# Linear attention into a tanh-shrink layer: the loads of the first batch move to a second queue, and the first batch's steps are reordered

## The chip, the cores and the metric

One core of one Trainium2 chip runs the whole program. The metric is the device time of one execution in microseconds (us), from start to end of the program; the kernel before takes 303.34 us (median of 3 runs, 302.98 to 303.97). The profile is one execution of its own, with a span of 301.5 us from its first to its last instruction; all times inside the program below are counted from the start of that span.

## The reference

Eight batches, eight heads, a sequence of 576 and a head size of 64 go through linear attention; its output, 4608 rows of 512, goes through two dense layers.

```python
phi = lambda x: np.where(x > 0, x, np.exp(x) - 1.0) + 1.0
q_p, k_p = phi(q), phi(k)                       # q, k, v: (8, 8, 576, 64) float32
kv  = np.einsum('bhsd,bhse->bhde', k_p, v)
z   = np.sum(k_p, axis=2)
num = np.einsum('bhsd,bhde->bhse', q_p, kv)
den = np.einsum('bhsd,bhd->bhs', q_p, z)[..., None] + 1e-06
x   = (num / den).transpose(0, 2, 1, 3).reshape(4608, 512)
h   = x @ w_in                                  # 512 x 2048
out = (h - np.tanh(h)) @ w_out                  # 2048 x 512
```

## The kernel before, in words

**The dense part.** The 4608 rows are handled in nine chunks `c` of 512. Layer 1 of a chunk is 16 groups `fi`, each of four 128x128 by 128x512 bf16 matmuls (line 275, `l1mm`); ScalarE takes tanh (line 280, `th`) and VectorE subtracts it (line 281, `gT`). Layer 2 is 16 groups of four matmuls (line 290, `l2mm`), which ScalarE copies out (line 295) and the SP queue stores (line 298). Weights and activations on TensorE are bf16.

**The attention part.** The attention of later batches is cut into small steps and hung between those groups, in the lists `s1` (after group `fi` of layer 1) and `s2` (after a quarter of a layer 2 group). The attention of batch 0 can't be hidden that way, since layer 1 of chunk 0 needs it: it is written out in front of the loop, behind 36 dummy matmuls on zeros (line 343) that keep TensorE's clock up. The order is by hand; each engine runs its own instructions in the order of the program, and waits on semaphores for the others.

The steps of batch 0, in the order of the program:

- `load_kq` (lines 85 and 89) and `load_v` (line 104) read q, k and v, which are float32 in memory, and turn them into bf16 on the way; they go out on the GpSimd queue. For batch 0, k and q come in four transfers each: half `i` (0 or 1) of the head pairs, and `hg` 0 or 1, which fill partitions 0 to 63 or 64 to 127. `load_wi` (line 110) and `load_wo` (line 114) bring the weights on the same queue. After the loads of w_in GpSimd builds `sel`, a selection matrix, with four `affine_select` (line 314).
- `phi`: exp on ScalarE (line 127, `e`), `max(x,0)+1` on VectorE (line 128, `r`), and the minimum of the two on VectorE (line 129, `kp` or `qp`): the same as the reference's function. It runs for k half 0, k half 1, q half 0, q half 1.
- `a_qT_pe(0, i)`: nine transposes of `qp` on TensorE (line 152) into two PSUM banks; the first is copied out by ScalarE (line 156), the second by VectorE (line 158).
- `a_kv_half(0, i)`: 18 matmuls (line 165) of kp with v and a column of ones, which give kv and z; VectorE masks them into `kz` (line 182).
- `a_den(0)`: 20 small matmuls (lines 190 and 194) give den, and VectorE takes the reciprocal (line 201, `rden`).
- `a_num_copy(0)`: one matmul per pair of heads `p` for the first 512 columns (line 220) and four small ones for the remaining 64 (line 223); ScalarE copies them to `ns` (lines 244 and 249). Pairs 0 and 2 need only half 0 of `kz` and `qT`, pairs 1 and 3 only half 1.
- `a_spread_pe(0)`: matmuls with `sel` (line 263) spread 1/den over the partitions, for two pairs at a time: pairs 0 and 1 into PSUM banks 0 to 3 (`bp_a`), pairs 2 and 3 into banks 4 to 7 (`bp_b`). They are float32, and each shows as two instructions in the profile.
- `a_scale(0, p)`: VectorE multiplies `ns` by the spread values into `xT` (line 268), the bf16 input of layer 1. Layer 1 of chunk 0 begins with groups `fi` 0 to 3 side by side in banks 0 to 3, all four for p = 0, then for p = 1, and so on, so that it can follow the scaling.

In chunk 1 the transposes of batch 2 hang behind groups 5 and 7 of layer 1, and use banks 6 and 7 (`attn`) in turn.

Of the kernel before, what the change touches and what calls it, by code (L numbers as in the profile page):

```python
# [11 lines left out]
F32 = mybir.dt.float32  # L12
BF16 = mybir.dt.bfloat16
# [5 lines left out]
def kernel(  # L19
# [9 lines left out]
    nc = tc.nc  # L29
    B, H, S, D = q.shape  # L30
# [3 lines left out]
    NP = H // 2  # L34
    NF = DF // 128
    NC = N // 512
    J = S // 64
# [25 lines left out]
    attn = Banks([6, 7])  # L63
# [14 lines left out]
    k_t, q_t = {}, {}  # L78

    def load_kq(b, src, store, name):  # L80
        t = kpool.tile([128, 2, 2, J, D], BF16, name=name)
        for i in range(2) if b == 0 else ():
            for hg in range(2):
                h0 = 4 * hg + 2 * i
                nc.gpsimd.dma_start(  # L85
                    out=t[64 * hg:64 * hg + 64, i].rearrange("p h j d -> p h (j d)"),
                    in_=src[b, h0:h0 + 2].rearrange("h (p j) d -> p h (j d)", j=J))
        for hg in range(2) if b > 0 else ():
            nc.gpsimd.dma_start(  # L89
                out=t[64 * hg:64 * hg + 64].rearrange("p i h j d -> p (i h) (j d)"),  # L90
                in_=src[b, 4 * hg:4 * hg + 4].rearrange("h (p j) d -> p h (j d)", j=J))
        store[b] = t

    def load_k(b):
        load_kq(b, k, k_t, "kraw")
# [4 lines left out]
    def load_v(b):  # L100
        for i in range(2):
            for hg in range(2):
                h0 = 4 * hg + 2 * i
                nc.gpsimd.dma_start(  # L104
                    out=v_b[b % 2][64 * hg:64 * hg + 64, i, 0:2].rearrange("p h j d -> p h (j d)"),
                    in_=v[b, h0:h0 + 2].rearrange("h (p j) d -> p h (j d)", j=J))

    def load_wi(g):
        f0 = g * (DF // 4)
        nc.gpsimd.dma_start(out=w_in_sb[:, :, f0:f0 + DF // 4],  # L110
                            in_=moe_w_in[:, f0:f0 + DF // 4].rearrange("(ko ki) f -> ki ko f", ki=128))
# [31 lines left out]
            out=qT_t[b].rearrange("p i j g t -> p (i j) (g t)"),  # L143
            in_=qp_t[b].rearrange("p i j h d -> p (i j h d)"))

    def a_qT_pe(b, i, banks):
        if i == 0:
            new_qT(b)
        for n, (j0, j1) in enumerate(((0, 5), (5, 9))):
            ps = banks().bitcast(BF16).rearrange("p (j t) -> p j t", t=128)  # L150
            for j in range(j0, j1):
                nc.tensor.transpose(ps[:, j - j0, :], qp_t[b][:, i, j].rearrange("p h d -> p (h d)"), ident)  # L152
            src = ps[:, 0:j1 - j0, :]
            dst = qT_t[b][:, i, j0:j1].rearrange("p j g t -> p j (g t)")
            if n == 0:
                nc.scalar.copy(dst, src)
            else:
                nc.vector.tensor_copy(dst, src)
# [57 lines left out]
    def num_mm(b, p, banks):  # L216
        kz, qT = kz_t[b], qT_t[b]
        ps = banks().rearrange("p (j t) -> p j t", j=8)
        if p < NP:
            nc.tensor.matmul(ps, kz[:, p // 2, p % 2, 0:128], qT[:, p % 2, 0:8, p // 2, :], start=True, stop=True)  # L220
        else:
            for a in range(NP):
                nc.tensor.matmul(ps[:, a, :], kz[:, a // 2, a % 2, 0:128], qT[:, a % 2, 8, a // 2, :],
                                 start=True, stop=True)
        return ps
# [11 lines left out]
                xT[:, :, S * b + 512:S * b + 576].rearrange("p a (t c) -> p a t c", t=4),  # L237
                ps[:, 0:NP, :].rearrange("p a (t c) -> p a t c", t=4), rdb[:, :, :, 8, :])

    def a_num_copy(b, banks):  # L240

        ns = rpool.tile([128, NP, J, 64], F32, name="ns", tag="rdb")
        ps = num_mm(b, NP, banks)
        nc.scalar.copy(ns[:, :, 8, :], ps[:, 0:NP, :])
        if b == 0:
            for p in range(NP):
                num_mm(b, p, banks)
            for p in (0, 2):
                nc.scalar.copy(ns[:, p:p + 2, 0:8, :].rearrange("p a j t -> p a (j t)"),
                               ps_all[:, 4 + p:6 + p, :])  # L250
        else:
            for p in range(NP):
                ps = num_mm(b, p, banks)
                nc.scalar.copy(ns[:, p, 0:8, :], ps)
        return ns

    def a_spread_pe(b, bank0, pairs):

# [45 lines left out]
    nc.scalar.activation(act0, zero[:, 0:1], AF.Exp)  # L304
    load_k(0)
    load_q(0)
    load_v(0)
    make_identity(nc, ident)
    for g in range(4):
        load_wi(g)  # L310
    nc.gpsimd.memset(sel, 0.0)
    for t in range(4):
        r = slice(32 * t, 32 * t + 32)
        nc.gpsimd.affine_select(
            out=sel[r], in_=sel[r], compare_op=ALU.not_equal, fill=1.0, base=0,
            channel_multiplier=1, pattern=[[-1, NP], [-4, 2], [0, 64]])
    load_k(1)
    load_wo(0)
    load_q(1)
# [19 lines left out]
        rest -= part  # L339


    for n in range(36):
        nc.tensor.matmul(ps_all[:, n % 4, :], zero[:, 0:128], zero, start=True, stop=True)  # L343
    for i in range(2):
        a_kphi(0, i)
# [3 lines left out]
    a_qT_pe(0, 0, side)  # L349
    a_kv_half(0, 0, kvb)  # L350
    a_qT_pe(0, 1, side)
    a_kv_half(0, 1, kvb)
    a_den(0, Banks([0]))
    ns0 = a_num_copy(0, Banks([1, 4, 5, 6, 7]))
    bp_a = a_spread_pe(0, 0, (0, 1))
    bp_b = a_spread_pe(0, 4, (2, 3))
    for p in range(NP):
        a_scale(0, p, ns0, (bp_a, bp_b)[p // 2], 144 * (p % 2))
    load_q(2)
    load_k(2)  # L360
    load_v(2)
# [1 line left out]
    for c in range(NC):  # L363
        gT = gpool.tile([128, NF, 512], BF16, name="gT")
        n1, n2 = c + 1, c + 2
        s1 = {i: [] for i in range(16)}
        s2 = {i: [] for i in range(16)}
        if c == 0:
            side = Banks([4, 5, 6, 7])
            sub = {}  # L370

            def spread1(h):
                sub["bp"] = a_spread_pe(1, 4, (2 * h, 2 * h + 1))
                for p in (2 * h, 2 * h + 1):
                    a_scale(1, p, sub["ns"], sub["bp"], 144 * (p % 2))

            s1[11].append(lambda: a_kphi(1, 0))
            s1[13].append(lambda: a_kphi(1, 1))
            s1[15].append(lambda: a_qphi(1, 0))
            s2[1].append(lambda: a_qphi(1, 1))  # L380
            s2[4].append(lambda: a_qT_pe(1, 0, side))
            s2[5].append(lambda: a_qT_pe(1, 1, side))
            s2[6].append(lambda: a_kv(1, side))
            s2[8].append(lambda: a_den(1, side))
            s2[9].append(lambda: (sub.update(ns=a_num_copy(1, side)), load_v(3)))
            s2[11].append(lambda: spread1(0))
            s2[13].append(lambda: spread1(1))
            s2[14].append(lambda: a_qphi(2, 0))
            s2[15].append(lambda: a_qphi(2, 1))
        elif n1 < B:  # L390
            s1[9 if c == 1 else 5].append(lambda: a_kv(n1, attn))
            s1[11 if c == 1 else 8].append(lambda: (a_den(n1, attn), a_spread(n1)))
            for p in range(NP + 1):
                s2[9 + p].append(lambda p=p: a_num(n1, p))
            if c + 3 < B:
                s1[10].append(lambda: load_v(c + 3))
        if c == 1:
            s1[1].append(lambda: a_kphi(2, 0))
            s1[3].append(lambda: (a_kphi(2, 1), load_k(3), load_q(3)))
            s1[5].append(lambda: a_qT_pe(2, 0, attn))  # L400
            s1[7].append(lambda: a_qT_pe(2, 1, attn))
        if c >= 1 and n2 < B:
            if c > 1:

                s1[0].append(lambda: (gate(gT, 0), load_k(n2), load_q(n2)))
            d = 4 if c == 1 else 2
            s2[d].append(lambda: a_kphi(n2, 0))
            s2[d + 2].append(lambda: a_kphi(n2, 1))
            s2[d + 4].append(lambda: a_qphi(n2, 0))
            s2[d + 6].append(lambda: (a_qphi(n2, 1), a_qT_dma(n2)))  # L410
        if c == 0:

            hs = [ps_all[:, fi, :] for fi in range(4)]
            first = Banks([4, 5, 6, 7, 0, 1, 2, 3])
            for p in range(NP):
                for fi in range(4):
                    l1mm(c, fi, hs[fi], p)
            for fi in range(4):
                l1act(fi, hs[fi], gT)
        for fi in range(4 if c == 0 else 0, NF):  # L420
            h = first() if c == 0 else dense()
            for p in range(NP):
                l1mm(c, fi, h, p)
            l1act(fi, h, gT)
            for f in s1[fi]:
                f()
        os_ = {}
        for s in range(16):

            (g, i) = divmod(s, 4) if c == 0 else (s % 4, s // 4)  # L430
            if g == 0:
                os_[i] = ps_all[:, i, :] if c == 0 else dense()
            l2mm(gT, os_[i], i, 4 * g, 4 * g + 4)
            if g == 3:
                evac(c, i, os_[i])
            for f in s2[s]:
                f()
# [30 lines left out]
```

## Time and profile before

| what | us |
|---|---|
| time, median of 3 | 303.34 |
| span of the profiled execution | 301.5 |
| TensorE busy | 292.2 (97%) |
| VectorE, ScalarE, GpSimd busy | 180.0, 149.6, 51.7 |
| dummy matmuls (line 343) | from 1.19 to 11.54 |
| first transposes of q (line 152) | at 12.13 |
| first matmul of layer 1 (line 275) | at 20.06 |
| first matmul of layer 2 (line 290) | at 33.87 |
| last matmul | ends at 296.6 |

TensorE looks busy from end to end, but its first 10 us are dummy work and the next 8 are the short steps of batch 0. The granted clock was 0.997 of full speed. The transfers keep the 16 DMA engines busy from 3 us to about 50 us. A line of the chain of waits gives a start, a duration, and what ran: an engine with the tile that it wrote and the line of the kernel, or a transfer. A line of the timeline gives a start, a duration, the engine, the line, and in square brackets the idle time ahead of it and what ended that. A line of the table of stretches gives for each engine its busy time and its number of instructions in that stretch, then the granted clock, the mean busy share of the DMA engines, and GB/s.

### The profile page before, as it was taken

How to read it: one execution, taken by the hardware profiler on the slowest of the kernel's cores; microseconds unless marked ns; L12 is line 12 of the kernel's file. 1: busy time of each engine (PE TensorE's matmuls, PEld its weight loads, DVE VectorE, ACT ScalarE, POOL GpSimd, SP SyncE). 2: the span in 40 equal slices, each digit the busy share in tenths (PEclk: the TensorE clock that was granted, in tenths of full speed). 3: DMA queues.
4: the chain of work that ended last, by engine and by line, in shares of the span. 5: the costliest groups of instructions: out<-in, count | busy, mean ns of one | idle time of the engine just before them, and what ended most of it. 6: DMA issues, size and time to landing. Idle time of an engine off the chain costs nothing.

```text
span 301.5 us, 4703 instructions
## 1 busy us (share of the span) xinstructions
PE 292.2 (97%) x1790; PEld 138.7 (46%) x1790; DVE 180.0 (60%) x304; ACT 149.6 (50%) x228; POOL 51.7 (17%) x91
## 2 busy tenths in 40 slices
PE   8989999979999999999999999999999999999993
PEld 3544454444445444544454445444544444444441
DVE  7658944887557854785478556865681467008500
ACT  3637914954735653566256625662562166136420
POOL 8863253051006000600050003000000000000000
PEclk9999999999999999999999999999999999999998
DMA  6999999677879776967787777477108310130033
GB/s 95 193 206 206 205 207 206 171 113 139 214 101 188 147 170 139 152 109 200 142 145 128 192 149 125 85 177 148 38 2 193 71 35 0 37 86 18 2 70 70
DMA packets 36406, 38.23 MB, mean 127 GB/s; under 512 B 14432, under 2 KB 31008, under 8 KB 35616
## 3 DMA queue, kind: packets, MB, share of 16 engines
q0 software_dynamic: 17600, 18.35, 37.7%
q1 hardware_dynamic: 18784, 19.58, 28.9%
q8 instruction: 14, 0.23, 0.3%
q14 instruction: 8, 0.07, 0.1%
HBM read 43.78 MB, written 9.55 MB: 177 GB/s over the span
## 4 chain that ended last, share of the span: by engine, by line
PE 86%; DMA 4%; DVE 3%; ACT 2%; POOL 1%; issue 1%; SPq 0%; DVEq 0%; ACTq 0%; POOLq 0%
PE ps_all L275 39%; PE ps_all L290 38%; PE ps_all L165 4%; DMA out_dram<-osb 2%; PE ps_all L220 2%; DMA qraw<-in_q_dram 2%; ACT e L127 1%; DVE gT L281 1%; PE ps_all L190 1%; ACT osb L295 1%; PE ps_all L152 1%; POOL kraw L85 1%; PE ps_all L263 1%; DVE qp L129 1%; DVE kp L129 1%
## 5 line engine op out<-in xcount | busy, mean ns | idle before, releaser
L290 PE MATMUL ps_all<-w_out_sb,gT 128*128 128x512 bf16 x576 | 131.6, 379 | 0.0
L281 DVE TENSOR_TENSOR gT<-ps_all,th 128x512 bf16<-128x512 f32 x144 | 96.9, 687 | 53.6 <-ACT th L280 53.2
L275 PE MATMUL ps_all<-xT,w_in_sb 128*128 128x512 bf16 x576 | 128.2, 379 | 0.3 <-DVE xT L268 0.3
L280 ACT ACTIVATE th<-ps_all 128x512 f32<-128x512 f32 x144 | 85.2, 599 | 51.5 <-PE ps_all L275 46.8
L275 PEld LDWEIGHTS <-w_in_sb 128*128 128x128 bf16 x576 | 55.3, 98 | 66.6 <-issue 1.3
L290 PEld LDWEIGHTS <-gT 128*128 128x128 bf16 x576 | 55.6, 98 | 65.7 <-issue 0.3
L295 ACT COPY osb<-ps_all 128x512 f32<-128x512 f32 x36 | 21.1, 587 | 79.7 <-PE ps_all L290 59.6
L231 DVE TENSOR_TENSOR xT<-ps_all,rdb 128x512 bf16<-128x512 f32 x24 | 16.4, 689 | 11.8 <-PE ps_all L220 11.8
L104 POOL DMA_DIRECT2D v<-in_v_dram x32 | 19.2, 616 | 19.0 <-PE ps_all L165 6.0
L127 ACT ACTIVATE e<-kraw 128x1152 bf16<-128x1152 bf16 x16 | 18.5, 1165 | 5.3 <-DMA kraw<-in_k_dram 5.3
L129 DVE TENSOR_TENSOR kp<-e,r 128x1152 bf16<-128x1152 bf16 x16 | 12.2, 760 | 14.1 <-ACT e L127 13.0
L127 ACT ACTIVATE e<-qraw 128x1152 bf16<-128x1152 bf16 x16 | 18.4, 1166 | 0.6 <-DMA qraw<-in_q_dram 0.6
L129 DVE TENSOR_TENSOR qp<-e,r 128x1152 bf16<-128x1152 bf16 x16 | 12.1, 758 | 7.8 <-ACT e L127 7.0
L286 POOL COPY g<-gT 1x1 bf16<-1x1 bf16 x4 | 0.7, 176 | 92.9 <-DVE gT L281 92.9
L165 PE MATMUL ps_all<-v,kp 64*128 64x192 bf16 x288 | 13.7, 243 | 0.0
L165 PEld LDWEIGHTS <-kp 64*128 64x128 bf16 x288 | 11.5, 94 | 3.3 <-issue 2.5
L343 PE MATMUL ps_all<-zero 128*128 128x512 bf16 x36 | 10.3, 460 | 1.2 <-DVE zero L302 1.2
L220 PE MATMUL ps_all<-qT,kz 128*128 128x512 bf16 x32 | 11.2, 379 | 0.0
L89 POOL DMA_DIRECT2D kraw<-in_k_dram x14 | 8.7, 628 | 11.0 <-ACT th L280 9.6
L89 POOL DMA_DIRECT2D qraw<-in_q_dram x14 | 8.8, 642 | 6.1 <-DVE r L128 6.1
L268 DVE TENSOR_TENSOR xT<-ns,ps_all 128x576 bf16<-128x576 f32 x8 | 5.6, 749 | 5.2 <-PE ps_all L263 5.2
L174 DVE TENSOR_TENSOR kz<-ps_all,mask 128x320 bf16<-128x320 f32 x14 | 6.2, 486 | 3.7 <-PE ps_all L165 3.7
(46 smaller groups left out, 92.3 us busy)
## 6 DMA issues: line engine op xcount, KB each, us to landing
out_dram<-osb SPq DMA_DIRECT2D x72, 128.0 KB
rdb<-ds SPq DMA_DIRECT2D x12, 576.0 KB
v<-in_v_dram POOLq DMA_DIRECT2D x32, 144.0 KB, 6.4
kraw<-in_k_dram POOLq DMA_DIRECT2D x14, 288.0 KB, 5.1
qraw<-in_q_dram POOLq DMA_DIRECT2D x14, 288.0 KB, 7.0
w_in_sb<-in_moe_w_in_dram POOLq DMA_DIRECT2D x4, 512.0 KB, 10.1
w_out_sb<-in_moe_w_out_dram POOLq DMA_DIRECT2D x4, 512.0 KB, 13.2
kraw<-in_k_dram POOLq DMA_DIRECT2D x4, 144.0 KB, 3.7
```

The source lines that it names most:

```text
L89: nc.gpsimd.dma_start(out=t[64 * hg:64 * hg + 64].rearrange("p i h j d -> p (i h) (j d)"), in_=src[b, 4 * hg:4 * hg + 4].rearrange("h (p j ...
L104: nc.gpsimd.dma_start(out=v_b[b % 2][64 * hg:64 * hg + 64, i, 0:2].rearrange("p h j d -> p h (j d)"), in_=v[b, h0:h0 + 2].rearrange("h (p ...
L127: nc.scalar.activation(e, x, AF.Exp)
L129: nc.vector.tensor_tensor(store[b][:, i].rearrange("p j h d -> p h j d"), e, r, ALU.min)
L165: nc.tensor.matmul(ps[hg], kp[r, i, j].rearrange("p h d -> p (h d)"), vt[r, i, :, j, :], start=(j == 0), stop=(j == J - 1))
L220: nc.tensor.matmul(ps, kz[:, p // 2, p % 2, 0:128], qT[:, p % 2, 0:8, p // 2, :], start=True, stop=True)
L231: nc.vector.tensor_mul(xT[:, p, S * b:S * b + 512].rearrange("p (j t c) -> p j t c", j=8, t=4), ps.rearrange("p j (t c) -> p j t c", t=4), ...
L275: nc.tensor.matmul(h, w_in_sb[:, p, fi * 128:(fi + 1) * 128], xT[:, p, c * 512:(c + 1) * 512], start=(p == 0), stop=(p == NP - 1))
L280: nc.scalar.activation(th, h, AF.Tanh)
L281: nc.vector.tensor_sub(gT[:, fi, :], h, th)
L290: nc.tensor.matmul(o, gT[:, fi, i * 128:(i + 1) * 128], w_out_sb[:, fi, :], start=(fi == 0), stop=(fi == NF - 1))
L295: nc.scalar.copy(osb, o)
```

## The change

It means to start layer 1 of chunk 0 earlier. Its parts:

- k and q of batch 0 are loaded as they are, as float32, by the SP queue, into two buffers of the pool that `ns` uses; they are no longer turned into bf16. v of batch 0 stays on GpSimd, which now builds `ident` and `sel` ahead of it.
- 29 dummy matmuls instead of 36.
- The numerators of pairs 0 and 2 of batch 0 are computed and copied out ahead of the second half of kv; the rest follows den. Each pair has a ScalarE copy of its own.
- 1/den of pair 0 is spread alone into banks 0 to 3, those of pairs 1, 2 and 3 together into banks 4 to 7, so that layer 1 can have banks 0 to 3 once pair 0 is scaled.
- In chunk 1 the transposes of batch 2 are hung singly, a half of each, behind groups 4, 5, 6 and 7 instead of in twos behind 5 and 7.

```diff
     def load_kq(b, src, store, name):
-        t = kpool.tile([128, 2, 2, J, D], BF16, name=name)
-        for i in range(2) if b == 0 else ():
+        if b == 0:
+            t = rpool.tile([128, 2, 2, J, D], F32, name=name + "0", tag="rdb")
+            for i in range(2):
+                for hg in range(2):
+                    h0 = 4 * hg + 2 * i
+                    nc.sync.dma_start(
+                        out=t[64 * hg:64 * hg + 64, i].rearrange("p h j d -> p h (j d)"),
+                        in_=src[b, h0:h0 + 2].rearrange("h (p j) d -> p h (j d)", j=J))
+        else:
+            t = kpool.tile([128, 2, 2, J, D], BF16, name=name)
             for hg in range(2):
-                h0 = 4 * hg + 2 * i
                 nc.gpsimd.dma_start(
...
-    def a_qT_pe(b, i, banks):
-        if i == 0:
+    def a_qT_pe(b, i, banks, parts=(0, 1)):
+        if i == 0 and 0 in parts:
             new_qT(b)
-        for n, (j0, j1) in enumerate(((0, 5), (5, 9))):
+        for n in parts:
+            j0, j1 = ((0, 5), (5, 9))[n]
...
-    def a_num_copy(b, banks):
-        ns = rpool.tile([128, NP, J, 64], F32, name="ns", tag="rdb")
-        ps = num_mm(b, NP, banks)
-        nc.scalar.copy(ns[:, :, 8, :], ps[:, 0:NP, :])
-        if b == 0:
-            for p in range(NP):
-                num_mm(b, p, banks)
-            for p in (0, 2):
-                nc.scalar.copy(ns[:, p:p + 2, 0:8, :].rearrange("p a j t -> p a (j t)"),
-                               ps_all[:, 4 + p:6 + p, :])
...
+    def a_num_copy(b, ns, p, banks):
+        ps = num_mm(b, p, banks)
+        if p < NP:
+            nc.scalar.copy(ns[:, p, 0:8, :], ps)
         else:
-            for p in range(NP):
-                ps = num_mm(b, p, banks)
-                nc.scalar.copy(ns[:, p, 0:8, :], ps)
-        return ns
+            nc.scalar.copy(ns[:, :, 8, :], ps[:, 0:NP, :])
...
     load_k(0)
     load_q(0)
-    load_v(0)
     make_identity(nc, ident)
-    for g in range(4):
-        load_wi(g)
     nc.gpsimd.memset(sel, 0.0)
...
+    load_v(0)
+    for g in range(4):
+        load_wi(g)
     load_k(1)
...
-    for n in range(36):
+    for n in range(29):
         nc.tensor.matmul(ps_all[:, n % 4, :], zero[:, 0:128], zero, start=True, stop=True)
...
     a_qT_pe(0, 1, side)
+    ns0 = new_ns(0)
+    for p in (0, 2):
+        a_num_copy(0, ns0, p, side)
     a_kv_half(0, 1, kvb)
     a_den(0, Banks([0]))
-    ns0 = a_num_copy(0, Banks([1, 4, 5, 6, 7]))
-    bp_a = a_spread_pe(0, 0, (0, 1))
-    bp_b = a_spread_pe(0, 4, (2, 3))
+    a_num_copy(0, ns0, NP, Banks([1]))
+    for p in (1, 3):
+        a_num_copy(0, ns0, p, side)
+    bp_a = a_spread_pe(0, 0, (0,))
+    bp_b = a_spread_pe(0, 4, (1, 2, 3))
     for p in range(NP):
-        a_scale(0, p, ns0, (bp_a, bp_b)[p // 2], 144 * (p % 2))
+        a_scale(0, p, ns0, bp_b if p else bp_a, 144 * (p - 1) if p else 0)
...
-            s1[5].append(lambda: a_qT_pe(2, 0, attn))
-            s1[7].append(lambda: a_qT_pe(2, 1, attn))
+            for n in range(4):
+                s1[4 + n].append(lambda n=n: a_qT_pe(2, n // 2, attn, (n % 2,)))
```

More of the change, by code (lines that the diff above doesn't have):

```diff
@@ L80, in load_kq @@
     def load_kq(b, src, store, name):
-        t = kpool.tile([128, 2, 2, J, D], BF16, name=name)
-        for i in range(2) if b == 0 else ():
+        if b == 0:
[8 more added lines that the diff above has]
+            t = kpool.tile([128, 2, 2, J, D], BF16, name=name)
             for hg in range(2):
-                h0 = 4 * hg + 2 * i
                 nc.gpsimd.dma_start(
[L86 to L91, printed above, removed]
+                    out=t[64 * hg:64 * hg + 64].rearrange("p i h j d -> p (i h) (j d)"),
+                    in_=src[b, 4 * hg:4 * hg + 4].rearrange("h (p j) d -> p h (j d)", j=J))
         store[b] = t
@@ L238, in a_num, with new_ns @@
                 ps[:, 0:NP, :].rearrange("p a (t c) -> p a t c", t=4), rdb[:, :, :, 8, :])
-    def a_num_copy(b, banks):
-        ns = rpool.tile([128, NP, J, 64], F32, name="ns", tag="rdb")
-        ps = num_mm(b, NP, banks)
-        nc.scalar.copy(ns[:, :, 8, :], ps[:, 0:NP, :])
-        if b == 0:
-            for p in range(NP):
-                num_mm(b, p, banks)
-            for p in (0, 2):
-                nc.scalar.copy(ns[:, p:p + 2, 0:8, :].rearrange("p a j t -> p a (j t)"),
-                               ps_all[:, 4 + p:6 + p, :])
-        else:
-            for p in range(NP):
-                ps = num_mm(b, p, banks)
-                nc.scalar.copy(ns[:, p, 0:8, :], ps)
-        return ns
+    def new_ns(b):
+        return rpool.tile([128, NP, J, 64], F32, name="ns", tag="rdb")
+    def a_num_copy(b, ns, p, banks):
+        ps = num_mm(b, p, banks)
+        if p < NP:
+            nc.scalar.copy(ns[:, p, 0:8, :], ps)
+        else:
+            nc.scalar.copy(ns[:, :, 8, :], ps[:, 0:NP, :])
     def a_spread_pe(b, bank0, pairs):
@@ L384, with num1 @@
             s2[8].append(lambda: a_den(1, side))
-            s2[9].append(lambda: (sub.update(ns=a_num_copy(1, side)), load_v(3)))
+            def num1():
+                sub["ns"] = new_ns(1)
+                for p in (NP, 0, 1, 2, 3):
+                    a_num_copy(1, sub["ns"], p, side)
+                load_v(3)
+            s2[9].append(num1)
             s2[11].append(lambda: spread1(0))
```

## The prediction

> **What bounds the kernel now.** I read the chain of waits first, then TensorE's waits, then the timeline of the first 21 us, then the table of stretches for the DMA engines. The chain, by start and duration:
>
> ```profile
> 4.27 5.77 DMA qraw<-in_q_dram
> ...
> 10.12 1.17 ACT e L127
> 11.29 0.02 issue
> 11.31 0.77 DVE qp L129
> ...
> 14.48 0.90 PE ps_all L165 x18
> 15.37 0.32 DVE kz L182
> ...
> 16.33 1.07 DVE rden L201
> 17.40 0.14 issue
> 17.54 0.95 PE ps_all L263 x14
> ...
> 18.59 1.43 DVE xT L268 x2
> 20.02 0.04 issue
> 20.06 13.97 PE ps_all L275 x64
> ```
>
> The head is paced by the transfers of k and q up to 10 us and then by a relay of short steps; from 20.06 the chain is TensorE, but for a stretch from 52.8 to 63.3 us. So what comes off the 20.06 comes off the end, if nothing later takes it back. TensorE's own waits say what else there is:
>
> ```profile
> PE ps_all L152 <- DVE qT L158: 1.1, 1, 1.1
> PE ps_all L152 <- ACT qT L156: 0.6, 1, 0.6
> PE ps_all L152 <- DVE qp L129: 0.6, 1, 0.6
> PE ps_all L275 <- DVE xT L268: 0.3, 1, 0.3
> ```
>
> The first two are batch 2's transposes at 61 to 63 us, the third is the end of the dummies (11.54) to the first transpose (12.13). In the timeline each exp and `r` of batch 0 starts when its transfer lands: k half 0 at 5.32, k half 1 at 8.66, q half 0 at 10.12, q half 1 at 11.59. VectorE is busy with memsets until 5.71.
>
> [...] with the same 2.36 MB read but 2.36 MB written instead of 1.18. [...] packets of 2048 B of a lone pair of stores, each from 64 partitions, took about 155 ns at 288 us (205 GB/s), but 84 ns at 55.5 us, where several stores of alternate halves stood in the queue. [...] The trace shows turns that favour GpSimd's: from 52.5 to 54.0 us its records hold 47 store packets against 203 load packets. [...] No fp32 form runs here; bf16 takes 0.45 [...].
>
> **Part by part.**
>
> *Loads.* The unknown is the rate. Both neighbours are in the table of stretches:
>
> ```profile
> 55.00:56.00 1.00, 1.00 (x6) 0.49 (x5) 0.64 (x2) 1.00 (x2) 0.00 (x0) 1.00 0.94 321
> 104.00:106.00 2.00, 2.00 (x11) 0.94 (x10) 1.74 (x4) 1.17 (x2) 0.00 (x0) 1.00 1.01 244
> ```
>
> (last column GB/s.) The first is stores of the SP queue, many in line, 64 partitions each; the second is two SP loads of 64 partitions (`rdb`), whose 1.18 MB needed 5.8 us in all, 203 GB/s. The eight loads here stand in line as the stores do, but write as `rdb` does; all `rdb` partitions read the same 9 KB, which k and q don't. So 205 to 390 (2304 B at the store's rate of 2048 B in 84 ns, times 16); I take 340. SP can issue at about 0.7 us (GpSimd's first transfer is at 1.24); one issue takes 0.56, less than the 0.9 that 295 KB need; first packets came 1.3 us after issue for `rdb`, so at 2.0. GpSimd's ident and sel take 0.5 + 0.56 + 2.84 = 3.9 from 1.24, so v goes out at 5.2, its first packets at 6.8 (1.6 later, as for k before), in number from about 7.3. By then 5.3 x 340 = 1.80 MB are in: k half 0 at 3.8, k half 1 at 5.5, q half 0 at 7.3. The last 0.56 MB share with v: at equal turns (95 + 91 ns a pair of packets, 16 engines: 198 GB/s) 2.8 us, so q half 1 lands at about 10.2, with 0.1 to finish, instead of 11.55. At 390 it is 9.0; at 205 with contended turns (about 150 GB/s) 15.8.
>
> *phi.* VectorE needs 0.75 + 0.76 per half, from 5.71: qp half 0 at 5.71 + 3 x 1.51 = 10.2, before 12.08. Half 1: exp at 10.25 to 11.4, then 0.8: 12.2, before 13.55. If transfers were no limit, VectorE would give it at 11.7. So exp and the fp32 cost of 4 x 0.3 lie beside the transfers, in part. The 29 dummies, seven fewer of 0.216, end at 10.03, ahead of qp, so they cost nothing; the clock stays.
>
> *num ahead of kv.* Two matmuls of 0.216 now stand before kv of half 1 on TensorE: +0.43 on the path, as den waits for kv. kz half 0 is there (it was at +2.3 after qp half 0, as TensorE arrives). In return only two pairs are left behind den, where TensorE waited 1.07 for the reciprocal anyway: nothing. ScalarE's copies after den are 0.37 + 2 x 0.61 = 1.6 instead of 2.3.
>
> *Spread alone.* Count from den's end (16.29 before): the reciprocal to +1.1, first spread +1.25. Before: 16 instructions (0.95), two scalings (1.43), layer 1 at +3.77, since banks 0 to 3 came free with pair 1. After: 8 instructions (0.28 + 7 x 0.045 = 0.6), pair 0 scaled at +2.66; but TensorE must first issue the other 24, to 1.25 + 0.28 + 31 x 0.045 = +2.93. The copy of pair 3 ends at +1.9, in time. Layer 1 at +2.95: gain 0.82. Pairs 1 to 3 are scaled at +3.4, +4.1, +4.8; layer 1 wants them at +3.8, +4.7, +5.5: no wait.
>
> *Sum.* qp half 1 1.35 earlier, +0.43, -0.82: 1.74 us, layer 1 at 18.3.
>
> *What could take it back.* w_in landed in quarters from 17.3 to 25.1 (issue plus landing); GpSimd's stream now runs about 2 us ahead, since its first 6 us moved 0.8 MB less than its later 404 GB/s of source would have, so no wait. v of batch 1 landed at 39.8 and is used at 41.05: 1.25 us of slack plus that lead. Removing k and q of batch 0 from GpSimd's queue hides no new wait, since GpSimd runs far ahead.
>
> *Chunk 1.* The split changes nothing in TensorE's work ahead of the last transposes, nor in VectorE's order; that wait is for VectorE's copy of the second bank (62.79 to 63.20), which still stands behind the same gT. The 0.6 wait goes, and the 1.1 becomes 1.7. Bounds 0 and 1.7; I take 0.
>
> **The rivals.**
>
> *VectorE paces phi* (loads at 390 or fair turns): qp half 1 at 11.7, gain 1.85 + 0.39 = 2.24, 301.1. For: stores at 84 ns. [...]
>
> [...] If GpSimd's queue takes two or three packets per packet of SP (as at 52.5), the last 0.56 MB move at 114 to 135 GB/s and q half 1 lands at 11.5 to 12.3: gain 0.4 to loss 0.4, no change, 303.3. With loads at 280 GB/s, 1.48 MB are in at 7.3, 0.88 MB at about 140 take 6.3: 13.6, a loss of 13.6 - 11.55 - 0.39 = 1.7, 305.0. This is the case on the other side. For: `rdb` six times at about 203 GB/s, the 47 against 203. Against: `rdb` is four packets per engine and transfer from one source.
>
> *Loads at 205 GB/s*: q half 1 at 15.8, loss 3.9, 307.2, and more if TensorE, idle from 10.0, loses clock.
>
> **How the numbers follow.** Forecast (gain 1.0 to 2.0) 0.38; VectorE-paced (2.0 to 2.6) 0.18; no change 0.12; turns lost (to +2.2) 0.18; 205 GB/s 0.14. Predicted 303.34 - 1.74 = 301.6. The range 300.7 to 305.5 leaves out the slow loads and a few of the best. Faster 0.56, same 0.12, slower 0.32.
>
> **What would show it.** Right: exp of q half 1 starts at about 10.3, qp half 0 ends at about 10.2, `r` takes 0.75, line 263 in one run of 1.7 us, first line 275 at about 18.3; a wait of 1.7 for line 158 at 60 us. Wrong: k half 1 landing after 7 us [...], q far behind k (turns), TensorE idle after its dummies, or a wait of line 165 for v at 39 us.

## The result, and the profile after

The changed kernel takes 307.16 us (median of 4 runs, 306.75 to 307.53), beside 303.48 us for the kernel before in the same comparison: a ratio of 1.012 with a 95% interval of 1.010 to 1.014. It is slower by 3.7 us, where 1.74 us less was forecast. In the profiles the first matmul of layer 1 starts at 23.55 instead of 20.06 us, and from there to the last matmul both kernels need the same: 276.5 us now and 276.6 before. The whole loss, 3.49 us in these two profiles, lies in the head, the part ahead of layer 1.

The chain of waits of the changed kernel, by start and duration; line 87 is the SP transfer, 131 exp, 133 `qp`, 157 the transposes, 225 num, 170 kv, 206 the reciprocal, 262 the spread, 267 the scaling, 274 layer 1:

```profile
4.81 0.61 SPq L87
5.46 9.19 DMA qraw<-in_q_dram
14.75 1.17 ACT e L131
15.95 0.77 DVE qp L133
16.77 1.14 PE ps_all L157 x9
17.91 0.85 PE ps_all L225 x2
18.76 1.02 PE ps_all L170 x18
...
20.74 1.07 DVE rden L206
21.95 0.71 PE ps_all L262 x6
22.75 0.77 DVE xT L267
23.55 13.97 PE ps_all L274 x64
```

The last of q is issued by 5.46 and arrives 9.19 us later. Each exp of batch 0 starts when its half of k or q has landed, so its start is used as the time of landing from here on. ScalarE's four exps (start, duration, what runs, the idle time ahead and what ended it):

```profile
5.96 1.17 ACT L131 ACTIVATE e<-kraw 128x1152 bf16<-128x1152 f32 x1 [3.73 <-DMA kraw<-in_k_dram]
...
8.54 1.16 ACT L131 ACTIVATE e<-kraw 128x1152 bf16<-128x1152 f32 x1 [1.42 <-DMA kraw<-in_k_dram]
...
11.56 1.16 ACT L131 ACTIVATE e<-qraw 128x1152 bf16<-128x1152 f32 x1 [1.85 <-DMA qraw<-in_q_dram]
...
14.75 1.17 ACT L131 ACTIVATE e<-qraw 128x1152 bf16<-128x1152 f32 x1 [2.03 <-DMA qraw<-in_q_dram]
```

Before, they started at 5.32, 8.66, 10.12 and 11.59, the last of them as

```profile
11.59 1.16 ACT L127 ACTIVATE e<-qraw 128x1152 bf16<-128x1152 bf16 x1 [0.31 <-DMA qraw<-in_q_dram]
```

k half 0 is 0.6 us later than it was and k half 1 no later; q half 0 is 1.4 us later and q half 1 3.2 us. The stretches of the changed kernel show two more things (last three columns: granted clock, DMA share, GB/s):

```profile
5.00:7.00 2.00, 2.00 (x10) 0.93 (x9) 1.33 (x7) 1.04 (x1) 2.00 (x4) 1.00 1.04 232
7.00:9.00 2.00, 2.00 (x11) 0.88 (x10) 1.20 (x2) 0.58 (x2) 2.00 (x4) 1.00 1.04 221
...
11.00:13.00 2.00, 0.00 (x0) 0.00 (x0) 1.01 (x2) 1.16 (x1) 0.52 (x1) 0.79 1.13 259
13.00:15.00 2.00, 1.43 (x15) 1.22 (x17) 0.77 (x2) 0.25 (x1) 0.72 (x2) 0.50 1.18 222
...
17.00:19.00 2.00, 2.00 (x17) 1.15 (x16) 0.93 (x4) 1.32 (x3) 0.61 (x1) 0.50 1.24 205
```

From 5 to 9 us the DMA engines are full, and they move only 221 to 232 GB/s of k and q. By the records of the packets (2304 B each) the middle one by duration takes 156 ns over all of k and q and 180 ns from 7 to 9 us. In the first us of the loads, up to 3.25, it takes 93; the slow ones set in behind that. And TensorE, which has nothing to do from 9.65 (the end of its 29 dummies) to 13.57, has half the clock (0.50) from 12.2 to 19.0 us: its transposes take 1.14 us instead of 0.68.

### The profile page after: what moved, and what is told of

It reads as the page before. It is cut to its first block, busy times and chain, and to the rows that moved or that the text cites. A ratio compares the mean times of both kernels' runs of the same rounds, so it can differ in the third digit from the quotient of the medians.

```text
span 305.0 us, 4695 instructions
## 1 busy us (share of the span) xinstructions
PE 291.7 (96%) x1783; PEld 138.8 (46%) x1783; DVE 181.2 (59%) x304; ACT 149.6 (49%) x230; POOL 47.4 (16%) x83
## 3 DMA queue, kind: packets, MB, share of 16 engines
q0 software_dynamic: 16448, 17.17, 34.6%
## 4 chain that ended last, share of the span: by engine, by line
PE 85%; DMA 5%; DVE 3%; ACT 2%; SPq 2%; issue 1%; DVEq 0%; ACTq 0%
PE ps_all L274 39%; PE ps_all L289 37%; PE ps_all L170 4%; DMA qraw<-in_q_dram 3%; DMA out_dram<-osb 2%; PE ps_all L225 2%; SPq L87 1%; ACT e L131 1%; DVE gT L280 1%; PE ps_all L195 1%; ACT osb L294 1%; PE ps_all L157 1%; PE ps_all L262 1%; DVE qp L133 1%; DVE kp L133 0%
## 5 line engine op out<-in xcount | busy, mean ns | idle before, releaser
L236 DVE TENSOR_TENSOR xT<-ps_all,rdb 128x512 bf16<-128x512 f32 x24 | 16.4, 690 | 11.8 <-PE ps_all L225 11.8
L131 ACT ACTIVATE e<-kraw 128x1152 bf16<-128x1152 bf16 (+1 forms) x16 | 18.5, 1165 | 5.1 <-DMA kraw<-in_k_dram 5.1
L131 ACT ACTIVATE e<-qraw 128x1152 bf16<-128x1152 bf16 (+1 forms) x16 | 18.4, 1166 | 3.9 <-DMA qraw<-in_q_dram 3.9
L225 PE MATMUL ps_all<-qT,kz 128*128 128x512 bf16 x32 | 11.8, 395 | 0.0
L157 PE MATMUL ps_all<-ident,qp 128*128 128x128 bf16 x54 | 5.3, 249 | 6.2 <-DVE qp L133 4.4
L342 PE MATMUL ps_all<-zero 128*128 128x512 bf16 x29 | 8.5, 463 | 1.2 <-DVE zero L301 1.2
L132 DVE TENSOR_SCALAR r<-qraw 128x1152 bf16<-128x1152 bf16 (+1 forms) x16 | 7.9, 491 | 2.3 <-DMA qraw<-in_q_dram 2.3
```

Of the source, the lines that this page charges most:

```text
L131: nc.scalar.activation(e, x, AF.Exp)
L236: nc.vector.tensor_mul(xT[:, p, S * b:S * b + 512].rearrange("p (j t c) -> p j t c", j=8, t=4), ps.rearrange("p j (t c) -> p j t c", t=4), ...
```

## The experiments

Three theories stood at the start. **Width**: the 64 partitions of an SP transfer of fp32 are what holds k and q to about 225 GB/s (221 to 232 above). **Turns**: v on GpSimd's queue takes the DMA engines from q. **Order**: the new order of the small steps costs more than it saves. A fourth, **bytes**, is that fp32 is slow because it writes twice as much, whatever the partitions.

### The old loads in the new order

```diff
-            t = rpool.tile([128, 2, 2, J, D], F32, name=name + "0", tag="rdb")
...
-                    nc.sync.dma_start(
...
+        t = kpool.tile([128, 2, 2, J, D], BF16, name=name)
...
+    load_v(0)
     make_identity(nc, ident)
+    for g in range(4):
+        load_wi(g)
     nc.gpsimd.memset(sel, 0.0)
...
-    for n in range(29):
+    for n in range(36):
```

> The changed kernel with the loads of the kernel before (k, q and v cast on GpSimd, sel built after them, 36 dummies); the other edits stay. If only the loads were at fault, exp of q half 1 starts at 11.6 again and layer 1 at about 19.7, since den to layer 1 takes 2.9 us instead of 3.8 and num ahead of kv costs 0.43: 0.4 us faster than before, about 303.1. If the new order of the small steps costs something itself, layer 1 starts after 20.1 and the kernel is no faster than before.

Measured: 302.74 us beside 303.33, ratio 0.998 (0.997 to 1.000). Layer 1 starts at 19.33. TensorE in this kernel (line 153 is the transposes, 166 kv, 221 num, 258 the spread, 270 layer 1):

```profile
13.55 0.68 PE L153 MATMUL ps_all<-ident,qp 128*128 128x128 bf16 x9
14.06 0.59 PE L221 MATMUL ps_all<-qT,kz 128*128 128x512 bf16 x2
14.59 0.92 PE L166 MATMUL ps_all<-v,kp 64*128 64x192 bf16 x18
...
17.72 1.40 PE L258 MATMUL ps_all<-rden,sel 32*128 32x144 f32 x32 [0.60 <-DVE rden L202]
19.33 1.89 PE L270 MATMUL ps_all<-xT,w_in_sb 128*128 128x512 bf16 x8 [0.20 <-DVE xT L263]
```

From the end of qp half 1 (13.32) to layer 1 it is 6.01 us, before 6.51 (13.55 to 20.06). The new order is sound, and saves 0.5; the theory of order falls.

### The new loads in the old order

```diff
-        t = kpool.tile([128, 2, 2, J, D], BF16, name=name)
...
+            t = rpool.tile([128, 2, 2, J, D], F32, name=name + "0", tag="rdb")
...
+                    nc.sync.dma_start(
...
-    load_v(0)
     make_identity(nc, ident)
-    for g in range(4):
-        load_wi(g)
     nc.gpsimd.memset(sel, 0.0)
...
+    load_v(0)
+    for g in range(4):
+        load_wi(g)
     load_k(1)
```

> The kernel before with the new loads alone (fp32 on SP, v on GpSimd behind sel); 36 dummies, old order of num, spread and transposes. If the loads are the fault, q half 1 lands at 14.7 as in the changed kernel, and layer 1 starts at about 20.06 + 3.2 = 23.2 if the dummies, which end at 11.5, keep the clock up, and near 24 if they don't: 306.6 to 307.5. If the order of the steps is the fault, it stays near 303.5.

Measured: 308.44 us beside 303.33, ratio 1.017 (1.015 to 1.019); exp of q half 1 starts at 15.16. Layer 1 starts only at 25.36, later than either guess: TensorE idles from 15.3 to 17.17 between the two halves, and the clock is half from 16.3 to 23.1 us in spite of the longer dummies, though no gap behind them is over 1.95 us. The loads alone are the fault, and they cost more here than in the changed kernel, whose order gives some back.

### v out of the way

```diff
+    fill = const.tile([128, 512], F32, name="fill")
+    for n in range(13):
+        nc.gpsimd.memset(fill, 0.0)
     load_v(0)
```

> The changed kernel with 13 memsets of an unused tile on GpSimd ahead of the loads of v, so that v is issued at about 11.5 us instead of 4.6 and k and q have the DMA engines to themselves. [...] it lands as in the changed kernel, at 14.7. If v's packets take turns from it after 9.5, q half 1 lands at about 2.3 + 2.36 MB / 228 GB/s = 12.7 and q half 0 near 10.3, k as before (5.96 and 8.54). The end of the kernel says nothing here, as v and w_in come later.

The first outcome there is that of the slow pace alone, the second that of v's share. Measured: v is issued at 13.67, after all of q. Its stretches, the same columns (the changed kernel has 221 in the first, and 235 in the second, where v has a share of it):

```profile
7.00:9.00 2.00, 2.00 (x11) 0.88 (x9) 1.29 (x3) 0.64 (x2) 1.83 (x4) 1.00 1.04 236
9.00:11.00 2.00, 0.85 (x4) 0.20 (x2) 1.04 (x2) 0.66 (x1) 1.83 (x4) 1.00 1.06 235
```

And the exps of q in the timeline of ScalarE:

```profile
11.01 1.16 ACT L131 ACTIVATE e<-qraw 128x1152 bf16<-128x1152 f32 x1 [1.35 <-DMA qraw<-in_q_dram]
...
13.42 1.16 ACT L131 ACTIVATE e<-qraw 128x1152 bf16<-128x1152 f32 x1 [1.25 <-DMA qraw<-in_q_dram]
```

The four exps start at 5.97, 8.49, 11.01 and 13.42, one every 2.5 us: 590 KB at 236 GB/s with nothing beside them. So both theories hold a part: against 11.59 before, the pace alone costs 1.83 us, and v's share another 1.33 (14.75 in the changed kernel). Each is a difference of two single executions: with the old loads q half 1 came at 11.59, 11.37 and 11.15 in three profiles (the kernel before, the one with the old loads and the one with the split alone), so a few tenths of 1.83 can be chance. The landing was 0.7 later than expected; the last packet ends at 12.65, 0.8 us ahead of the exp. The end (309.85, one run) is later because v is: TensorE waited 3.3 us for it.

### All partitions at once

```diff
+            flat = src[b].rearrange("h s d -> (h s d)").rearrange("(x p f) -> x p f", x=4, f=J * D)
             for i in range(2):
-                for hg in range(2):
-                    h0 = 4 * hg + 2 * i
-                    nc.sync.dma_start(
-                        out=t[64 * hg:64 * hg + 64, i].rearrange("p h j d -> p h (j d)"),
-                        in_=src[b, h0:h0 + 2].rearrange("h (p j) d -> p h (j d)", j=J))
+                for h in range(2):
+                    nc.sync.dma_start(out=t[:, i, h].rearrange("p j d -> p (j d)"), in_=flat[2 * i + h])
```

> The changed kernel with each of the eight SP transfers of k and q spread over all 128 partitions (2304 B per partition and transfer, 295 KB each as before). The tokens land in another order, so q and k of batch 0 are other values and the output isn't the reference's; the instructions and waits are the same. [...] k half 1 lands before 7 us and q half 1 before 11: 301.6 to 302.5. If doubled bytes or shared turns limit, it lands as in the changed kernel: 307.

The first outcome there is that of the theory of width. Measured: 302.21 us beside 303.33, ratio 0.996 (0.995 to 0.997). Same bytes, same packets of 2304 B, same queue, but each transfer reaches all 128 partitions. This kernel leaves out the matching order of v and w_in, so it shows what the width is worth and can't replace the other:

```profile
3.00:5.00 2.00, 2.00 (x6) 0.63 (x5) 1.81 (x2) 0.51 (x1) 1.87 (x4) 1.00 0.97 304
5.00:7.00 2.00, 2.00 (x6) 0.76 (x5) 1.72 (x8) 0.66 (x1) 2.00 (x4) 1.00 0.94 280
7.00:9.00 2.00, 2.00 (x10) 0.87 (x9) 1.17 (x2) 1.12 (x1) 2.00 (x4) 1.00 1.04 392
```

The middle packet takes 93 ns instead of 156, and 392 GB/s are reached. The theory of bytes falls: with the bytes unchanged, the width alone raised the rate. k half 1 landed at 7.9, later than the 7 expected, since the rate sagged to 280 from 5 to 7 us, for which I have no cause; q half 1 landed at 11.8. The profile is of an execution of 304.41 us, the longest of 19 (the others took 301.32 to 302.88): besides the sag it had half the clock from 13.8 to 17.3 us, although TensorE was never idle for more than 0.94 us behind its dummies, and layer 1 started at 21.21. So its stretches show that the width raises the rate, and the 302.21 what that is worth; its landings are not the usual ones.

### Two queues for the two halves

```diff
-                    nc.sync.dma_start(
+                    (nc.sync, nc.scalar)[hg].dma_start(
```

> The changed kernel with the transfers to partitions 64 to 127 of k and q on ScalarE's queue, those to partitions 0 to 63 on SP's. Same bytes, packets and cast-free loads. [...] packets of both halves now mix, packets take nearer 93 ns than 182, k half 1 is in before 7 us and q half 1 at about 10: layer 1 near 18.3, 301.6 to 302.2. If it is the doubled bytes whatever the partitions, or the turns that GpSimd's queue takes, landing stays at 8.5 for k and 14.7 for q and the time at 307.

The first outcome there is that of the theory of width. Measured: 305.48 us beside 303.33, ratio 1.007 (1.005 to 1.009). The expectation failed for k: half 1 landed at 8.7, and from 5 to 9 us the rate was 225 to 237 GB/s, as before. The packet records say why: the two queues were not mixed but served in bursts, from 5.0 to 5.5 us for example 54 packets of ScalarE's queue beside one of SP's, and the middle packet from 4 to 9 us took 168 ns. Only from 9 to 10.5 us were both served about evenly (98 and 92 packets); there it took 128 ns, and the rate rose (the two stretches from 9 to 11 us, v from 10.5):

```profile
9.00:10.00 1.00, 1.00 (x6) 0.49 (x5) 0.82 (x2) 0.83 (x1) 1.00 (x3) 1.00 1.08 288
10.00:11.00 1.00, 0.50 (x3) 0.00 (x1) 0.62 (x1) 0.00 (x0) 0.74 (x1) 1.00 1.04 304
```

That fits the theory of width: the rate was 288 and 304 GB/s while both halves were written at a time, beside the 225 to 237 ahead of that. The last packet of q came at 12.5, ahead of the changed kernel's 14.0, also as v's packets came only at 10.5; exp of q half 1 started at 13.57, held last by VectorE. Why the queues were served in bursts, is open.

### More dummies

```diff
-    for n in range(29):
+    for n in range(46):
```

> The changed kernel with 46 dummies instead of 29: they end at about 13.3, just ahead of the first transposes. Transfers are untouched, q half 1 lands at 14.7. If the half clock from 12.4 to 19.2 us is what made the relay behind q 0.7 us longer than forecast, the clock stays at 1.0 and layer 1 starts at 22.8 instead of 23.55: about 306.4. If the relay is long for another reason, it stays at 307.2.

Measured: 306.14 us beside 303.41, ratio 1.010 (1.008 to 1.012), and in the same stretches as above the clock is whole (1.00):

```profile
13.00:15.00 2.00, 2.00 (x31) 1.47 (x29) 0.61 (x2) 0.17 (x1) 0.61 (x1) 1.00 1.18 229
15.00:17.00 2.00, 0.34 (x9) 0.16 (x4) 1.56 (x3) 1.58 (x2) 1.36 (x2) 1.00 1.24 208
17.00:19.00 2.00, 2.00 (x37) 1.35 (x35) 1.07 (x5) 1.67 (x3) 0.61 (x1) 1.00 1.24 205
```

```profile
14.84 1.16 ACT L131 ACTIVATE e<-qraw 128x1152 bf16<-128x1152 f32 x1 [2.19 <-DMA qraw<-in_q_dram]
...
22.70 9.66 PE L274 MATMUL ps_all<-xT,w_in_sb 128*128 128x512 bf16 x43 [0.20 <-DVE xT L267]
```

With q half 1 at 14.84, qp half 1 ends at 16.79 and layer 1 starts at 22.70: a relay of short steps of 5.91 us, beside 6.83 in the changed kernel (16.72 to 23.55). The lost clock cost 0.9, and 1.0 in the times (306.14 beside 307.16).

### Full width for the reference's output

```diff
+    def flat(src, b):
+        return src[b].rearrange("h s d -> (h s d)").rearrange("(x p f) -> x p f", x=4, f=J * D)
...
+            for x in range(4):
+                nc.sync.dma_start(out=t[:, x // 2, x % 2].rearrange("p j d -> p (j d)"), in_=flat(src, b)[x])
...
-        nc.gpsimd.dma_start(out=w_in_sb[:, :, f0:f0 + DF // 4],
-                            in_=moe_w_in[:, f0:f0 + DF // 4].rearrange("(ko ki) f -> ki ko f", ki=128))
+        for hg in range(2):
+            for h in range(2):
+                nc.gpsimd.dma_start(
+                    out=w_in_sb[64 * h:64 * h + 64, 2 * hg:2 * hg + 2, f0:f0 + DF // 4],
+                    in_=moe_w_in[:, f0:f0 + DF // 4].rearrange("(i h g e) f -> h g e i f", i=2, h=2, g=2)[h, hg])
...
-    for n in range(29):
+    for n in range(38):
```

> The reference's output, with the heads dealt out so that every transfer of k, q and v is 128 partitions wide (head 2x + hg in place of 4hg + x), the rows of w_in loaded to match (16 transfers of 64 partitions instead of 4 of 128), and 38 dummies. k and q still fp32 on SP. [...] q half 1 lands at about 11.8 as with full width alone, and layer 1 starts at about 20: 302.9 or a little less, and 1 us better if v waits less. If the doubled bytes were the fault, about 307.

The first outcome there is that of width and the lost clock as the causes. Measured: 302.42 us beside 303.41, ratio 0.997 (0.995 to 0.998), about 1 us faster than the kernel before. k and q of later batches come in one transfer each instead of two, and v in two instead of four; the body takes as long as before (276.9 us). The rates:

```profile
5.00:7.00 2.00, 2.00 (x10) 0.94 (x9) 1.72 (x8) 0.66 (x1) 2.00 (x4) 1.00 1.02 363
7.00:9.00 2.00, 2.00 (x11) 0.93 (x10) 1.90 (x3) 1.61 (x2) 2.00 (x3) 1.00 1.05 346
```

q half 1 and layer 1:

```profile
10.17 1.16 ACT L127 ACTIVATE e<-qraw 128x1152 bf16<-128x1152 f32 x1 [0.46 <-DMA qraw<-in_q_dram]
...
18.55 13.97 PE L270 MATMUL ps_all<-xT,w_in_sb 128*128 128x512 bf16 x62 [0.20 <-DMA w_in_sb<-in_moe_w_in_dram]
```

q half 1 lands at 10.2, as the prediction had forecast it for 64 partitions; k half 1 only at 7.1 where 5.5 was forecast. Nothing sags to 280 here (363 from 5 to 7 us). Layer 1's wait ends with w_in, but at 0.20 us it is no longer than that for xT in the kernel with the old loads. The 38 dummies are a few too many: they hold TensorE until 11.33, though qp half 0 is there at 10.73, and the transposes of half 1 start 0.5 us after their qp.

### Full width for cast loads

Against the kernel just above, which sends them as fp32 on SP:

```diff
-            t = rpool.tile([128, 2, 2, J, D], F32, name=name + "0", tag="rdb")
+            t = kpool.tile([128, 2, 2, J, D], BF16, name=name)
...
-                nc.sync.dma_start(out=t[:, x // 2, x % 2].rearrange("p j d -> p (j d)"), in_=flat(src, b)[x])
+                nc.gpsimd.dma_start(out=t[:, x // 2, x % 2].rearrange("p j d -> p (j d)"), in_=flat(src, b)[x])
```

> The changed kernel with k and q of batch 0 cast on GpSimd as before, but all transfers of k, q and v 128 partitions wide (heads dealt out as in the kernel above), 36 dummies. [...] width makes no difference and q half 1 lands at 11.4: 302.7, as with the old loads. [...] it lands before 10 and the time is 301.5.

The first outcome there (302.7) is that of a cast load that gains nothing from width, the second (301.5) that of one that does. Measured: 311.11 us beside 303.41, ratio 1.026 (1.024 to 1.028), and no answer on the time: v and w_in are issued ahead of `sel` again, so `sel` stands behind the sixteen transfers of w_in on GpSimd, and TensorE waited 4.9 us for it. exp of q half 1 started at 10.87. The second form, against this one, builds `sel` behind the first quarter of w_in:

```diff
-    for g in range(4):
-        load_wi(g)
+    load_wi(0)
     nc.gpsimd.memset(sel, 0.0)
...
+    for g in range(1, 4):
+        load_wi(g)
     load_k(1)
```

> The reference's output, heads dealt out, all transfers of k, q and v 128 partitions wide and cast on GpSimd, with sel built behind the first quarter of w_in so that it is ready in time; 36 dummies. If width alone decides, q half 1 lands near 10.9 and layer 1 starts near 18.9, as close to the fp32 full-width kernel as its 0.7 us later landing allows: about 302.5. If a cast load gains nothing from width, 302.7 as with the old loads.

Measured: 305.01 us beside 303.08, ratio 1.006 (1.004 to 1.008): layer 1 started at 19.80, but layer 2 then waited 2.1 us for w_out, which this order delays. (This profile is of an execution of 307.07 us, the longest of six.) exp of q half 1 started at 11.41; with 64 partitions it did at 11.15, 11.37 and 11.59. So 10.87 and 11.41 with full width are hardly apart from what the old loads give by chance, and a gain from width isn't shown. The cast load had been writing only about 200 GB/s (295 KB every 1.47 us before), below the 236 that fp32 got on 64 partitions. What holds the cast load at that rate, no run here shows.

### The split in chunk 1 alone

```diff
-            s1[5].append(lambda: a_qT_pe(2, 0, attn))
-            s1[7].append(lambda: a_qT_pe(2, 1, attn))
+            for n in range(4):
+                s1[4 + n].append(lambda n=n: a_qT_pe(2, n // 2, attn, (n % 2,)))
```

> The kernel before with the transposes of batch 2 hung singly behind groups 4 to 7 and nothing else changed. If the last wait is set by VectorE's order, TensorE's two waits there become 1.0 and 0.76 in place of 0.6 and 1.1, with the same end: 303.4, no change. If the split saves the wait, up to 1.7 us faster, 301.7.

Measured: 303.50 us beside 303.08, ratio 1.001 (1.000 to 1.002): no gain. TensorE's waits there:

```profile
PE ps_all L153 <- ACT qT L157: 1.0, 1, 1.0
PE ps_all L153 <- DVE qT L159: 0.8, 1, 0.8
```

Together they are as long as the 0.6 and 1.1 of the kernel before (the waits for lines 156 and 158 there).

## Why the prediction was wrong

**The step that failed** is the rate of the loads: "So 205 to 390 [...]; I take 340." It was 236 with nothing beside them, and 221 to 232 in the changed kernel. The prediction had two neighbours in the trace, stores at 84 ns a packet and the `rdb` loads at 203 GB/s, and took the faster one because eight transfers stand in line. Its own table had the answer: the line of the `rdb` loads reads 244 GB/s while they run; the 203 is their bytes over all of 5.8 us. At full width the same bytes went at 346 to 363 with the heads dealt out. Why the stores at 55 us, also from 64 partitions each, took 84 ns a packet while these loads took 156, is open: the packets were faster (128 ns) where two queues wrote both halves at a time, but no run shows what sets that.

**The turns.** "At equal turns" was the author's estimate, and near the truth once v was being served: from 11.0 to 13.5 us the records hold 184 packets of q beside 185 of v. (The forecast's 47 store packets against 203 are 56 against 196 when counted by their starts; they were no guide to this.) But at the low rate 0.8 of the 2.36 MB was left when v came, a third instead of a quarter, and sharing the engines cost 1.33 us. v's start was off too: issued at 4.64, its first packets came at 8.8, not at 6.8. That delay helped q.

**The landing.** The sum allowed 0.1 from the last packet to exp. In the changed kernel it is 0.8 (13.97 to 14.75), and 0.5 to 0.9 for q half 1 in the other kernels with loads on SP where the exp waited for them. This term alone would have taken some 0.7 of the forecast gain of 1.74.

**phi.** The 0.75 for `r` in fp32 was the author's estimate; in bf16 the one at 10.57 us in the kernel before took 0.45 (line 128). In fp32 it took 0.76 (0.98 for k half 1), but hid in the waits for k and q: nothing on the path.

**num ahead and spread alone** were sized right. In the kernel with the old loads qp to den's end is 3.15 beside 2.74, so num costs 0.41 (0.43 forecast); den's end to layer 1 is 2.86 (2.95 forecast, 3.77 before). Net 0.5 for 0.39.

**The dummies.** "So they cost nothing; the clock stays" failed with the loads: with four idle us behind them the clock was lost, at a cost of 0.9. The rival had named this.

**Chunk 1** was right in its sum and wrong in its parts: the 0.6 did not go and the 1.1 did not become 1.7, as was said, but the two waits are 1.0 and 0.8, in the changed kernel too.

**The sum.** q half 1 lands 1.83 later by the pace and 1.33 by v's share; the new order makes the relay behind it 0.60 shorter, and the half clock makes it 0.92 longer: 3.48 of the 3.49 measured. These parts are steps along one chain, so they have to add up; what shows them is that each of the four was taken away alone. Against the forecast, layer 1 starts 5.2 us later (+3.49 where -1.74 was said), and 4.5 of that is the landing of q half 1: 3.16 later where 1.35 earlier was said. The rival "loads at 205 GB/s" (q at 15.8, 307.2) came closest in time, by luck: its q came 1 us too late, and its figure had no lost clock, which it only named as a possible extra; the two cancel.

## What to carry to other kernels

Before moving a load from one queue to another, ask what it writes and to how many partitions: here a cast load to 64 partitions wrote about 200 GB/s and gained nothing clear from full width, while the same load in fp32, with twice the bytes to write, came at 236 and at full width at 346 to 363. When a trace offers two neighbours for an unknown rate, look first at the one that shares the direction and the destination, and read its rate while it runs: here it was off by 3%, and the other by 65%. And what shortens the filler of an engine is to be tied to the arrival that it waits for, since a late arrival then costs the clock as well (0.9 us here). How long a gap may be, these runs don't settle: the clock fell to 0.50 with gaps of 3.9 us, with two of under 2, and in one execution with none over 0.94.

## What the runs showed that I had not expected

While SP's loads stood in line, v's first packets came 4.2 us after their issue (4.64 to 8.79). With nothing ahead of it, a load on GpSimd's queue took 1.4 us to its first packet (k in the kernel before, 1.24 to 2.65) and 1.5 (v in the kernel with v out of the way, 13.67 to 15.16). After that start the two queues shared about evenly (184 packets beside 185 from 11.0 to 13.5 us). From layer 1's first matmul to the last, the kernel takes 276.5 to 276.9 us in eight of the ten other profiles too, whatever was done to the head (278.6 and 280.6 in the two with full-width cast loads).
